# Transposing the next lane pair's x0 into DRAM ahead of the lane switch, in a Strassen cross-network kernel

## The chip, the cores and the metric

One core of one Trainium2 chip. The metric is the device time of one execution, in microseconds (us). The kernel before the change took 2412.36 us in the median of its first three runs (2412.25 to 2421.04).

## The reference

```python
B, F, D, L = 16384, 100, 16, 6          # Din = min(F * D, 1024) = 1024
# x0: (16384, 1024) bf16, ws: (6, 1024, 1024) bf16, bs: (6, 1024) bf16
def reference(x0, ws, bs):
    x = x0
    for l in range(6):
        proj = einsum('bd,de->be', x, ws[l]) + bs[l]
        x = x0 * proj + x
    return x
```

## The kernel before

The batch is cut into eight *lane pairs* (`lp`) of two *lanes* of 1024 rows. All six layers of a pair run with the activations transposed in SBUF: features on partitions, batch in the free dimension. A *unit* is one layer of one lane, so a pair has twelve units. Each layer's product is a Strassen scheme (seven half-size products, two of them split once more), fed by a ring of ten weight tiles of 512 KB each, nine per layer. Three of these nine are plain quarters of `ws`. The other six are sums that the first pair computes and stores in DRAM (`Lc`).

At the *lane switch* the last layer of a pair overlaps the first layer of the next. Each lane has four quarters of x0 (512 batch rows by 512 features, 512 KB). In the switch eight quarters of x0 come in and eight quarters of the result (`xf`) go out, each through a DMA transpose.

```python
def w_src(l, pid):                                   # where a weight tile is loaded from
    # ... pid 1, 2, 4: a quarter of ws[l], "(k p) e -> p k e": rows of 1 KB
    return Lc[l, CIDX[pid]].rearrange("p (k e) -> p k e", k=KH)     # rows of 4 KB

def prefetch():                                      # load as soon as a ring slot is free
    while st["next"] < len(keys) and can_alloc(st["next"]):
        # ...
        st["dma"] = nc.sync.dma_start(t_[:], w_src(key[1], key[2]))

def load_x0(lp, lane, eh, n):
    r0 = lp * LB + lane * PR + n * NB
    nc.sync.dma_start_transpose(out=q(x0L[lane], eh, n), in_=x0[r0:r0 + NB, eh * H:(eh + 1) * H])

def store_quarter(lp, lane, eh, n, xf):
    # ... dst = the quarter of xL
    nc.sync.dma_start_transpose(out=dst, in_=xf[:].rearrange("r j k p -> r (j k p)"))
    nc.sync.dma_start(out[...], q(xL[lane], eh, n)...)

def finish(c, add, eh, n):                           # a quarter of a layer is done
    tt(c, c, add, ADD)
    tt(c, c, q(x0T, eh, n), MULT)
    if nxt_x0:                                       # last layer, and a next pair exists
        load_x0(lp + 1, lane, eh, n)                 # x0T's quarter was read for the last time
    x_out(c, eh, n)                                  # last layer: makes xf, calls store_quarter
# ... tail_a does the same for a lane's last two quarters (eh = 1)
```

All these DMAs are issued by SyncE, in order. Only the accumulations `xL += c` of the middle layers come from GpSimd.

## Time and profile before

| | before |
|---|---|
| median of 3 runs | 2412.36 us |
| profiled span | 2414.6 us |
| mean distance of lane switches | 297.8 us |
| twelve undisturbed units (estimate, 12 x 23.4) | 281 us |
| TensorE at half clock, without the end of the run | 65 us |

The distance of switches is taken from the trace: from the first matmul that reads the new x0 in one pair to that in the next, mean of six. The half clock is the sum of the stretches at 0.5 in the trace's record of the granted clock.

The head of the profile's page gives the span, and each engine's busy time, its share and its instructions:

```profile
span 2414.6 us, 32963 instructions
PE 2286.9 (95%) x12912; PEld 1269.5 (53%) x12912; DVE 2116.1 (88%) x2096; ACT 1783.9 (74%) x2485; POOL 110.7 (5%) x133
```

The view of windows compares one switch with a steady stretch. Columns: the stretch and its length, busy us of each engine with its instructions, the granted clock, the mean busy share of the 16 DMA engines, GB/s. (The share counts packets' own times, which overlap a little, so a full engine shows about 1.0 to 1.2.)

```profile
core 0: us, PE busy (x) PEld busy (x) DVE busy (x) ACT busy (x) POOL busy (x), PEclk, DMA share, GB/s
577.70:645.20 67.50, 56.76 (x311) 30.70 (x310) 49.47 (x50) 43.00 (x61) 0.00 (x0) 0.95 1.02 241
400.00:590.00 190.00, 190.00 (x1108) 108.15 (x1107) 176.29 (x174) 150.95 (x212) 12.90 (x15) 1.00 0.58 154
```

In steady layers TensorE is busy all the time. In the switch it loses 11 of 67 us, and the DMA engines are full. The timeline of TensorE in that switch shows for which data it waited (in brackets: idle us before, and what ended it):

```profile
610.01 0.61 PE L259 MATMUL XB<-x0L,wp 128*128 128x256 bf16 x4 [1.26 <-DMA wp<-in_ws_dram]
612.49 0.61 PE L259 MATMUL XB<-ti,wp 128*128 128x256 bf16 x4 [1.86 <-DMA wp<-Lc]
...
620.41 1.04 PE L247 MATMUL XA<-x0L,wp 128*128 128x512 bf16 x4 [1.69 <-DMA wp<-Lc]
...
632.14 1.04 PE L259 MATMUL XB<-ti,wp 128*128 128x256 bf16 x4 [5.93 <-DMA wp<-Lc]
632.97 1.91 PE L247 MATMUL XA<-t,wp 128*128 128x512 bf16 x4
```

Every wait is for a weight tile. After the longest one, four 512-column matmuls take 1.91 us; at full clock the same four take 1.04 us. The timeline of the SyncE queue says where the weights were (start, us in the queue's hands, line, output<-input):

```profile
593.12 5.48 SPq L150 DMA_TRANSPOSE x0L<-in_x_dram  x2
598.70 4.56 SPq L155 DMA_TRANSPOSE xL<-xf  x2
...
604.20 0.49 SPq L100 DMA_DIRECT2D wp<-in_ws_dram  x1
...
606.00 2.07 SPq L100 DMA_DIRECT2D wp<-Lc  x2
608.17 5.33 SPq L150 DMA_TRANSPOSE x0L<-in_x_dram  x1
613.59 2.41 SPq L155 DMA_TRANSPOSE xL<-xf  x1
616.05 1.42 SPq L100 DMA_DIRECT2D wp<-Lc  x2
...
620.06 5.18 SPq L150 DMA_TRANSPOSE x0L<-in_x_dram  x1
625.34 2.43 SPq L155 DMA_TRANSPOSE xL<-xf  x1
627.86 1.02 SPq L100 DMA_DIRECT2D wp<-Lc  x2
```

A plain load leaves the queue in 0.5 to 1.0 us. A transpose holds it for 2.3 to 5.3 us, and the last weights that TensorE waits for are issued at 627.86, behind four transposes of x0 and four of `xf` in this list.

### The profile page before, as it was taken

The numbers are of one execution on the slowest core, as the hardware profiler recorded it, in microseconds if no ns is written. First come the engines' busy times: TensorE is split into PE (matmuls) and PEld (weight loads), VectorE is DVE, ScalarE is ACT, GpSimd is POOL, SyncE is SP. The second block draws the span as 40 slices with busy tenths as digits, with TensorE's granted clock in tenths as the row PEclk, the third lists the DMA queues.
The fourth block names the chain that finished last, engine by engine and source line by source line (L and its number), as shares of the span: only waits on it lengthen the run. The fifth ranks groups of instructions, "written<-read, shape, count | busy, mean of one in ns | idle before, by whom it ended". The sixth has DMA issues, their size and how long they took to land.

```text
span 2414.6 us, 32963 instructions
## 1 busy us (share of the span) xinstructions
PE 2286.9 (95%) x12912; PEld 1269.5 (53%) x12912; DVE 2116.1 (88%) x2096; ACT 1783.9 (74%) x2485; POOL 110.7 (5%) x133
## 2 busy tenths in 40 slices
PE   6999989999899997999989999899998999989997
PEld 3454545555455554555545555455554555545553
DVE  6998879998899988999879998799987999889997
ACT  4777767777677785787767887677776878768775
POOL 0000000000000000000000000000000000000000
PEclk9999999999999999999999999999999999999998
DMA  7465695557954579545784558845588456874566
GB/s 200 137 188 136 161 236 139 148 131 179 240 150 126 135 183 237 147 122 147 191 230 130 131 149 197 218 126 131 153 201 222 114 136 165 208 197 123 147 172 144
DMA packets 439899, 400.10 MB, mean 166 GB/s; under 512 B 276416, under 2 KB 386496, under 8 KB 439744
## 3 DMA queue, kind: packets, MB, share of 16 engines
q1 hardware_dynamic: 421312, 330.89, 49.0%
q0 software_dynamic: 18432, 67.12, 14.4%
q8 instruction: 101, 1.65, 0.3%
q14 instruction: 54, 0.44, 0.1%
HBM read 211.29 MB, written 52.43 MB: 109 GB/s over the span
## 4 chain that ended last, share of the span: by engine, by line
PE 77%; DVE 15%; DMA 5%; SPq 1%; issue 1%; ACT 1%; DVEq 0%; ACTq 0%
PE pA L247 35%; PE XA L247 23%; PE XB L259 19%; DVE t L63 4%; DVE D L63 3%; DVE ti L63 3%; DMA xL<-xf 3%; DMA x0L<-in_x_dram 2%; DVE S L63 2%; SPq L150 1%; DVE xf L63 1%; DVE xL L63 1%; DVE Q L63 1%; ACT P5s L239 1%; DMA wp<-in_ws_dram 0%
## 5 line engine op out<-in xcount | busy, mean ns | idle before, releaser
L247 PEld LDWEIGHTS <-wp 128*128 128x128 bf16 x7712 | 759.0, 99 | 773.8 <-issue 46.6
L247 PE MATMUL pA<-t,wp 128*128 128x512 bf16 x3104 | 780.2, 381 | 0.0
L259 PEld LDWEIGHTS <-wp 128*128 128x128 bf16 x5040 | 494.9, 99 | 333.8 <-DMA wp<-Lc 51.3
L239 ACT CAST F<-XB 128x1024 bf16<-128x1024 f32 x360 | 364.3, 1012 | 291.0 <-PE XB L259 284.4
L259 PE MATMUL XB<-ti,wp 128*128 128x256 bf16 x2880 | 436.9, 275 | 52.4 <-DMA wp<-Lc 45.5
L247 PE MATMUL XA<-t,wp 128*128 128x512 bf16 x1536 | 400.6, 385 | 2.4 <-DMA wp<-Lc 2.4
L247 PE MATMUL XA<-xL,wp 128*128 128x512 bf16 x1280 | 326.8, 379 | 2.3 <-ACT P5s L239 2.3
L247 PE MATMUL pA<-xL,wp 128*128 128x512 bf16 x1280 | 328.5, 379 | 0.0
L242 ACT ACTIVATE U3s<-pA,b_all 128x512 bf16<-128x512 f32 x384 | 264.4, 688 | 39.4 <-PE pA L247 19.0
L239 ACT CAST G<-XB 128x512 bf16<-128x512 f32 x360 | 211.7, 588 | 106.5 <-PE XB L259 105.2
L242 ACT ACTIVATE P1s<-pA,b_all 128x512 bf16<-128x512 f32 x384 | 266.0, 693 | 26.3 <-PE pA L247 18.5
L242 ACT ACTIVATE U2s<-pA,b_all 128x512 bf16<-128x512 f32 x384 | 266.1, 693 | 14.4 <-PE pA L247 5.1
L239 ACT CAST S<-XA 128x1024 bf16<-128x1024 f32 x192 | 194.3, 1012 | 64.1 <-PE XA L247 64.1
L239 ACT CAST P5s<-XA 128x1024 bf16<-128x1024 f32 x192 | 195.3, 1017 | 50.1 <-DVE D L63 30.8
L63 DVE TENSOR_TENSOR D<-D,x0L 128x4096 bf16<-128x4096 bf16 x96 | 220.0, 2292 | 13.3 <-ACT D L242 9.4
L63 DVE TENSOR_TENSOR t<-xL 128x4096 bf16<-128x4096 bf16 x80 | 183.4, 2293 | 23.4 <-DMA xL<-S 14.7
L63 DVE TENSOR_TENSOR t<-xL,t 128x2048 bf16<-128x2048 bf16 x160 | 194.9, 1218 | 0.0
L63 DVE TENSOR_TENSOR xL<-D,xL 128x4096 bf16<-128x4096 bf16 x64 | 146.7, 2292 | 6.6
L63 DVE TENSOR_TENSOR S<-S,U2s 128x2048 bf16<-128x2048 bf16 x96 | 117.2, 1221 | 31.8 <-ACT S L239 31.5
L305 POOL DMA_DIRECT2D xL<-Q x64 | 55.2, 863 | 1905.9 <-ACT U3s L242 862.2
L259 PE MATMUL XB<-t,wp 128*128 128x256 bf16 x1008 | 139.3, 275 | 0.0
L63 DVE TENSOR_TENSOR D<-P5s,U3s 128x2048 bf16<-128x2048 bf16 x96 | 117.3, 1222 | 24.4 <-ACT U3s L242 24.4
(43 smaller groups left out, 1752.0 us busy)
## 6 DMA issues: line engine op xcount, KB each, us to landing
wp<-Lc SPq DMA_DIRECT2D x252, 512.0 KB, 4.6
wp<-in_ws_dram SPq DMA_DIRECT2D x139, 512.0 KB, 5.9
xL<-Q POOLq DMA_DIRECT2D x64, 512.0 KB, 5.7
xL<-S POOLq DMA_DIRECT2D x64, 512.0 KB, 6.4
out_dram<-xL SPq DMA_DIRECT2D x64, 512.0 KB, 3.8
Lc<-wp SPq DMA_DIRECT2D x36, 512.0 KB, 5.0
w<-in_ws_dram SPq DMA_DIRECT2D x12, 512.0 KB, 7.7
x0L<-in_x_dram SPq DMA_TRANSPOSE x64, 5.4
```

The costliest lines, as they stand in the source:

```text
L63: return nc.vector.tensor_tensor(out=out, in0=in0, in1=in1, op=op)
L150: nc.sync.dma_start_transpose(out=q(x0L[lane], eh, n), in_=x0[r0:r0 + NB, eh * H:(eh + 1) * H])
L239: nc.scalar.copy(out=dst, in_=src)
L242: nc.scalar.activation(out=dst, in_=src, func=IDENT, bias=bias_col(eh, m), scale=1.0)
L247: nc.tensor.matmul(dst, lhsT=w_[:, k, m * P:(m + 1) * P], rhs=b_[:, k, :], start=(start and k == 0), stop=(k == KH - 1), skip_group_check= ...
L259: nc.tensor.matmul(dst[:, m * NQ:(m + 1) * NQ], lhsT=wv[:, k, m * P:(m + 1) * P], rhs=b_[:, k, :], start=(start and m == 0 and k == 0), st ...
L305: nc.gpsimd.dma_start(q(xst, eh, n), c, accum_op=ADD)
```

## The change

Intent: take the x0 transposes out of the switch. In layers 1 to 4 of each pair, each unit transposes one quarter of the next pair's x0 into an SBUF buffer and stores it in DRAM (`x0s`) in the layout that SBUF wants. The switch then only fetches 4 KB rows. Beside this, the weights 1, 2 and 4 are also copied into `Lc`, so that all later loads of weights read 4 KB rows. The staging pool gives up one buffer to make room. Core of the diff (pool and index changes and the startup's `w_save` cut):

```diff
+    x0s = dram.tile([2, 2, 2, 2, P, KH * NB], BF16, name="x0s")
...
+    def w_save(l, pid, t_):
+        nc.sync.dma_start(Lc[l, CIDX[pid]], t_[:].rearrange("p k e -> p (k e)"))
...
-            st["dma"] = nc.sync.dma_start(t_[:], w_src(key[1], key[2]))
+            if key[0] == 0:
+                nc.sync.dma_start(t_[:], w_src(key[1], key[2]))
+                if key[2] in (1, 2):
+                    w_save(key[1], key[2], t_)
+            else:
+                nc.sync.dma_start(t_[:].rearrange("p k e -> p (k e)"), Lc[key[1], CIDX[key[2]]])
...
+    def pre_x0(lp, lane, eh, n):
+        r0 = lp * LB + lane * PR + n * NB
+        xs = late["xf"].tile([P, KH, KH, P], BF16, name="xf")
+        nc.sync.dma_start_transpose(out=xs[:].rearrange("p a b r -> p a (b r)"), in_=x0[r0:r0 + NB, eh * H:(eh + 1) * H])
+        nc.sync.dma_start(x0s[lp % 2, lane, eh, n], xs[:].rearrange("p a b r -> p (a b r)"))
+
+    def fetch_x0(lp, lane, eh, n):
+        nc.sync.dma_start(q(x0L[lane], eh, n).rearrange("p k b -> p (k b)"), x0s[lp % 2, lane, eh, n])
...
             if nxt_x0:
-                load_x0(lp + 1, lane, eh, n)
+                fetch_x0(lp + 1, lane, eh, n)          # the same in tail_a
...
         prefetch()
+        if 1 <= l <= 4 and lp + 1 < NLP:
+            i_ = (l - 1) * 2 + lane
+            pre_x0(lp + 1, i_ // 4, i_ % 2, (i_ // 2) % 2)
```

More of the change, by code (lines that the diff above doesn't have):

```diff
@@ L49 @@
     stage = stage_ctx.enter_context(tc.tile_pool(name="stage", bufs=2))
-    late = {}
-    CIDX = {5: 0, 6: 1, 7: 2, 3: 3, "2i": 4, "4i": 5}
+    stage1 = stage_ctx.enter_context(tc.tile_pool(name="stage1", bufs=1))
+    late = {"xf": stage1}
+    CIDX = {5: 0, 6: 1, 7: 2, 3: 3, "2i": 4, "4i": 5, 1: 6, 2: 7, 4: 8}
     Lc = dram.tile([L, len(CIDX), P, KH * H], BF16, name="Lc")
+    x0s = dram.tile([2, 2, 2, 2, P, KH * NB], BF16, name="x0s")
     pA = [psum.tile([P, NB], FP32, name=f"pA{i}") for i in range(KH)]
@@ L73, in w_src @@
             return wl[H:D, H:D].rearrange("(k p) e -> p k e", p=P)
-        return Lc[l, CIDX[pid]].rearrange("p (k e) -> p k e", k=KH)
+        raise KeyError(pid)
+    def w_save(l, pid, t_):
+        nc.sync.dma_start(Lc[l, CIDX[pid]], t_[:].rearrange("p k e -> p (k e)"))
     USE = [1, 2, "2i", 5, 3, 6, 4, "4i", 7]
@@ L108, in load_stage @@
         nc.sync.dma_start(w22[l][:], w_src(l, 4))
-        w12[l] = stage.tile([P, KH, H], BF16, name="w12")
+        w_save(l, 4, w22[l])
+        w12[l] = stage1.tile([P, KH, H], BF16, name="w12")
         nc.sync.dma_start(w12[l][:], ws[l][0:H, H:D].rearrange("(k p) e -> p k e", p=P))
@@ L135, in combo @@
             tt(s_[7], a11, a21, SUB)
-        nc.sync.dma_start(Lc[l, CIDX[pid]].rearrange("p (k e) -> p k e", k=KH), t_[:])
+        w_save(l, pid, t_)
         if pid == "4i":
@@ L195 @@
     nc.sync.dma_start(t_[:], w_src(0, 1))
+    w_save(0, 1, t_)
     load_stage(0)
@@ L373, in tail_a @@
                 for n in (1, 0):
-                    load_x0(lp + 1, lane, 1, n)
+                    fetch_x0(lp + 1, lane, 1, n)
             if last_layer:
```

## The prediction

> **What bounds it now.** The table of engines has TensorE busy 2286.9 us of 2414.6. By stretches (windows), from 400 to 590 us and in every steady stretch like it TensorE is busy 190.0 of 190 us at full clock, VectorE about 176. One layer of one lane takes 23.4 us, twelve take 281. But in the chain of waits the lane switches (marked by the transposes back, `xL<-xf`, at 598.7, 1193.8, 1492.7, 1792.4 ...) come every 298 us: each of the seven loses about 17 us, some 120 in all. From 590 to 700 us TensorE is idle 12.4 us; the list of waits gives most of it to late weights (45.5 us behind `wp<-Lc` and 18.3 behind `wp<-in_ws_dram` in one group over the run, longest 7.8). Most of the rest is half clock after the gaps (four 512-column matmuls in 1.9 us instead of 1.03; one granted-clock stretch of 6.8 us at 0.5). That agrees with the Trainium skill, "TensorE: Matmul & The Clock Gate", Part 1: after an idle window of about 3.4 us the array runs at half rate.
>
> **Why the weights are late.** All transfers but the accumulations go through the one in-order SyncE queue. In its timeline the next lanes' nine weights, wanted from 591 us on, are issued from 604.2 to 630.2, behind transposes: those of x0 hold the queue 2.1 to 5.3 us each, 2.74 where two follow one another, those of `xf` 2.0 to 2.4. DMA's share is 0.95 to 1.13 from 589 to 632 us, so transfers are the limit too. Estimated occupancy of a switch: 8 x 2.74 (x0) + 8 x 2.35 (xf) + 17 x 1.5 (weights and stores, at the 350 GB/s that traced plain loads reach) = 66 us; the trace takes 577.7 to 645. (The skill, "DMA: Bandwidth & Descriptors", Latency and other measured facts, gives 261 GB/s for a transpose; this trace shows 190 to 225.)
>
> **What the change does.** Per switch, eight x0 transposes become plain 4 KB-row loads: 0.4 us of queue and about 1.4 of transfer each (estimate from `wp<-Lc`), so -11 us of DMA and -18 of queue. Three `in_ws` weights per layer become `Lc` rows (4.6 us to landing instead of 5.9): about -1.5 us. Added: a transpose and a 512 KB store in eight of twelve units, about +4.1 us of DMA per 23.4 us, where the share is 0.42 to 0.73, so it fits; 18 more `Lc` stores in the first lane pair, three near the start, where DMA is at 0.97.
>
> **On the path.** The switch stays near the DMA limit (about 54 us of traffic), so I expect 12 of its 17 us back: the long weight wait and the half clock behind it. 7 x 12 = -84. Against it: +3 at the start, +6 for accumulations delayed in steady layers (VectorE already waits up to 1.4 us for `xL<-S`, with 1.7 us slack a unit).
>
> **Predicted: 2337 us, range 2305 to 2380.** Faster by over 2%: 0.81; within 2%: 0.16; slower: 0.03.
>
> **Signs.** Switch period 298 -> about 286 us; TensorE's waits for `wp` from 76 us to under 30; half-clock stretches at switches mostly gone; steady stretches still 100% TensorE, DMA share up by about 0.15; nine weights issued before about 612 in switch time; VectorE's wait for `xL<-xf` (95 us) at least halved.
>
> **What would make it wrong.** A store waiting for its transpose to land holds weights up in steady layers; hoisted transposes fall into the switch's end; accumulations slowed so VectorE (93% busy) becomes the limit; or `xf`, not x0, holds the queue, and only 5 us per switch come back.

## More of the kernel before

The framework that builds the program chooses SyncE's order. It need not keep the program's order: a DMA that waits for little can be issued well ahead of its place, as the queue after the change will show. The order of TensorE, ScalarE and VectorE is fixed by the program.

## The result, and the profile after

The changed kernel took 2378.29 us in the median (2375.51 to 2379.37, four runs) against 2413.18 for the kernel before in the same rounds. The ratio is 0.9847, with a 95% interval of 0.9824 to 0.9869. A ratio here is the mean time of one kernel's runs over that of the other's of the same rounds, so it is not quite the ratio of the medians. The gain is 1.5%, about 35 us, where 75 us were predicted; the time lies just under the top of the predicted range of 2305 to 2380, and the class "faster by over 2%" was missed.

| | before | after |
|---|---|---|
| profiled span | 2414.6 us | 2373.7 us |
| first matmul starts | 11.1 us | 13.7 us |
| mean distance of lane switches | 297.8 us | 291.5 us |
| half clock, without the end of the run | 65 us | 41 us |

From the start of the second pair to the end, before took 2414.6 - 312.4 = 2102.2 us and after 2373.7 - 314.8 = 2058.9 us: 43.3 us less over seven switches, or 6.2 us each. The whole gain came from there. (The two profiled executions took 2416.68 and 2375.51 us, 6 us further apart than the medians; by the medians, with the later start added back, it is (34.9 + 2.6) / 7 = 5.4 us each.)

The head of the page after the change. (Of the matmuls 253 records are missing; the weight loads, x12912 as before, show that none was left out. Busy times of TensorE are therefore read 1 to 2% low.)

```profile
span 2373.7 us, 32873 instructions
PE 2264.8 (95%) x12659; PEld 1267.6 (53%) x12912; DVE 2114.4 (89%) x2096; ACT 1784.9 (75%) x2485; POOL 110.7 (5%) x133
```

Windows: the switch, the 54 us behind it, and a steady stretch, columns as above.

```profile
core 0: us, PE busy (x) PEld busy (x) DVE busy (x) ACT busy (x) POOL busy (x), PEclk, DMA share, GB/s
573.00:636.00 63.00, 56.40 (x306) 30.89 (x311) 51.31 (x52) 43.33 (x62) 0.00 (x0) 0.95 0.99 272
636.00:690.00 54.00, 53.16 (x305) 30.32 (x310) 52.76 (x54) 42.02 (x59) 1.72 (x2) 1.00 1.01 267
690.00:850.00 160.00, 158.97 (x910) 90.78 (x928) 146.67 (x147) 127.46 (x180) 12.03 (x14) 1.00 0.57 158
```

The switch is shorter but its DMA engines are as full as before (0.99). The transposes ahead are not spread over the layers as the program has them: they need nothing but a free buffer, so the queue runs all eight right behind the switch (share 1.01 from 636 to 690), and the steady stretch shows no extra traffic. TensorE is still busy for 53.2 of these 54 us.

TensorE's timeline in the switch, with its waits:

```profile
604.74 0.61 PE L281 MATMUL XB<-ti,wp 128*128 128x256 bf16 x4 [0.65 <-DMA wp<-Lc]
...
612.02 1.04 PE L269 MATMUL XA<-x0L,wp 128*128 128x512 bf16 x3 [1.04 <-DMA wp<-Lc]
...
622.41 1.04 PE L281 MATMUL XB<-ti,wp 128*128 128x256 bf16 x4 [4.59 <-DMA wp<-Lc]
623.24 1.91 PE L269 MATMUL XA<-t,wp 128*128 128x512 bf16 x4
```

The small waits shrank. The long one, for the weights of the same group, is still 4.6 us and still brings the half clock. The SyncE queue:

```profile
586.83 1.70 SPq L171 DMA_DIRECT2D x0L<-x0s  x2
588.94 6.49 SPq L176 DMA_TRANSPOSE xL<-xf  x2
...
598.42 2.09 SPq L110 DMA_DIRECT2D wp<-Lc  x2
600.60 0.40 SPq L171 DMA_DIRECT2D x0L<-x0s  x1
601.09 5.93 SPq L176 DMA_TRANSPOSE xL<-xf  x1
607.08 1.06 SPq L110 DMA_DIRECT2D wp<-Lc  x2
...
612.82 5.47 SPq L176 DMA_TRANSPOSE xL<-xf  x1
618.39 1.01 SPq L110 DMA_DIRECT2D wp<-Lc  x2
```

Where x0's transposes held the queue 5.2 to 5.3 us, `xf`'s now hold it 5.5 to 5.9, and before they took 2.4. The transpose of `xf` is the same instruction, so most of its 5.5 to 5.9 us is not its own cost. The reading that fits is back-pressure: the full DMA engines take a transpose only slowly, and the next one in line inherits that time. No run isolates this. Part of the queue's time did come back: in this switch the transposes and fetches of x0 together with the transposes of `xf` held it for 47.1 us before and 37.8 us after.

The packets of the trace give the DMA work of one switch: their times summed and divided by the 16 engines. (The window after holds part of a first transpose ahead.)

```
                            before 577 to 646            after 573 to 636
256 B packets (transposes)  32768, 44.8 us = 16 x 2.80   17580, 24.0 us
1 KB packets                 4824, 15.6 us                3584, 11.8 us = 7 x 1.68
4 KB packets                  768,  8.9 us                2176, 26.3 us = 17 x 1.55
```

So 512 KB cost 2.80 us as a transpose and 1.55 us as 4 KB rows. A whole switch (eight quarters in, eight out, eight stores, nine weights) comes to about 72 us before and 62 us after.

### The profile page after: what moved, and what is told of

Read it like the earlier page. It is cut to its first block, busy times and chain, and to the rows that moved or that the text cites. A ratio compares the mean times of both kernels' runs of the same rounds, so it can differ in the third digit from the quotient of the medians.

```text
span 2373.7 us, 32873 instructions
## 1 busy us (share of the span) xinstructions
PE 2264.8 (95%) x12659; PEld 1267.6 (53%) x12912; DVE 2114.4 (89%) x2096; ACT 1784.9 (75%) x2485; POOL 110.7 (5%) x133
## 4 chain that ended last, share of the span: by engine, by line
PE 75%; DVE 15%; DMA 6%; issue 2%; ACT 1%; SPq 1%; DVEq 0%; ACTq 0%; POOLq 0%
PE pA L269 34%; PE XA L269 22%; PE XB L281 18%; DVE t L65 4%; DMA xL<-xf 4%; DVE D L65 3%; DVE ti L65 3%; DVE S L65 2%; DMA x0L<-x0s 1%; DVE xL L65 1%; DVE Q L65 1%; DVE xf L65 1%; SPq L161 0%; DMA xL<-S 0%; DMA wp<-Lc 0%
## 5 line engine op out<-in xcount | busy, mean ns | idle before, releaser
L269 PE MATMUL pA<-t,wp 128*128 128x512 bf16 x2982 | 758.7, 381 | 6.4
L269 PE MATMUL XA<-t,wp 128*128 128x512 bf16 x1474 | 386.1, 385 | 3.7 <-DMA wp<-Lc 0.5
L269 PE MATMUL pA<-xL,wp 128*128 128x512 bf16 x1254 | 323.2, 379 | 1.3
L65 DVE TENSOR_TENSOR t<-xL 128x4096 bf16<-128x4096 bf16 x80 | 183.4, 2293 | 41.6 <-DMA xL<-S 28.5
L65 DVE TENSOR_TENSOR Q<-Q,P1s 128x2048 bf16<-128x2048 bf16 x96 | 117.6, 1225 | 19.7 <-ACT Q L261 10.9
```

Of the source, the lines that this page charges most:

```text
L65: return nc.vector.tensor_tensor(out=out, in0=in0, in1=in1, op=op)
L269: nc.tensor.matmul(dst, lhsT=w_[:, k, m * P:(m + 1) * P], rhs=b_[:, k, :], start=(start and k == 0), stop=(k == KH - 1), skip_group_check= ...
```

## The experiments

The theories, as they stood before the first run. **A (order):** weights are late because they stand in the in-order queue behind transposes that are slow or not ready. **B (DMA work):** the switch is as long as the DMA engines need for its transfers; order only decides who waits. **C:** the transposes ahead, run right behind the switch, eat part of the gain. "Period" is the mean distance of switches; medians are given with that of the kernel before in the same rounds.

### The weight copies alone, and x0 alone

The first is the change with `load_x0` in place of `fetch_x0` and no `pre_x0`:

```diff
-                fetch_x0(lp + 1, lane, eh, n)
+                load_x0(lp + 1, lane, eh, n)        # the same in tail_a; pre_x0 and x0s removed
```

> The kernel before with one part of the change alone: all nine weights per layer come from the row copies; x0 is still transposed in the switch. Theory A (weights stand in the in-order queue behind transposes that are not ready, so the moment of issue decides): the x0 transposes are still there, nearly nothing comes back, 2400 to 2415 us, switch period 296 to 298 us. Theory B (the DMA engines are full in the switch): only about 1.5 us of traffic per switch goes, about 2400 us. Both say that this part is small; if more than 15 us come from it, both are wrong about x0.

Measured: 2414.86 us (before 2415.09), ratio 1.0001 [0.9987, 1.0016], period 297.5. The 4 KB rows for three of nine weights gave nothing.

The second is the change with weights 1, 2 and 4 read from `ws` as before, and no copies of them:

```diff
-                nc.sync.dma_start(t_[:].rearrange("p k e -> p (k e)"), Lc[key[1], CIDX[key[2]]])
+                if key[2] in (1, 2, 4):
+                    nc.sync.dma_start(t_[:], w_src(key[1], key[2]))
+                else:
+                    nc.sync.dma_start(t_[:].rearrange("p k e -> p (k e)"), Lc[key[1], CIDX[key[2]]])
```

> The change without its weight copies: x0 is transposed ahead and fetched as rows, weights 1, 2 and 4 come from the input in 1 KB pieces as before. Theories A and B: nearly the whole gain stays, 2375 to 2390 us, period 292 to 294 us. The sum of the gains of this run and of the rows-only run should be near the 35 us of the whole change.

Measured: 2377.07 us (before 2415.09), ratio 0.9842 [0.9825, 0.9858], period 292.2. The whole gain is x0's.

### No transposes ahead after the first pair (wrong result)

```diff
-        if 1 <= l <= 4 and lp + 1 < NLP:
+        if 1 <= l <= 4 and lp == 0:                  # and fetch_x0 always reads x0s[1, ...]
```

> The change, but only the first lane pair transposes x0 ahead; later switches fetch the same stale rows, so the result is wrong on purpose. All added steady traffic of the later pairs is gone, the switch itself is unchanged. Theory C (the transposes ahead, which the queue runs in the 50 us right after the switch, eat part of the gain): period 288 to 290 us, 2355 to 2365 us. Theories A and B: the time is lost in the switch, period stays at 292 us, 2372 to 2380 us.

Measured: 2376.63 us (before 2415.09), period 291.6; the result is wrong, as meant. Removing the added transposes and stores from six of the seven pairs that have them gives nothing back. Theory C falls: they are free where they run.

### The switch's weights from the GpSimd queue

```diff
-                nc.sync.dma_start(t_[:].rearrange("p k e -> p (k e)"), Lc[key[1], CIDX[key[2]]])
+                eng = nc.gpsimd if key[1] == 0 else nc.sync
+                eng.dma_start(t_[:].rearrange("p k e -> p (k e)"), Lc[key[1], CIDX[key[2]]])
```

> The change, but the nine weights that a switch needs (first layer of each later lane pair) are issued from the GpSimd queue, which has no other work there, so that they no longer stand behind the transposes of xf. The bytes moved are the same. Theory A (order): the 4.6 us wait at the tenth group and the half clock after it go, weights are issued when their slot comes free, period 284 to 287 us, 2325 to 2345 us. Theory B (DMA engines full, share 0.97 to 1.02 from the switch's start): issuing earlier only delays something else, period 290 to 293, 2365 to 2385 us.

Measured: 2469.83 us (before 2415.09), ratio 1.0218 [1.0192, 1.0244], period 304.2. Neither theory expected a loss of this size. The weights did go out early, eight of them from 601.5 to 616.7 us, and took 11.8 us to land (the median of all 63 in the run). The SyncE queue and VectorE in that stretch:

```profile
602.42 22.26 SPq L177 DMA_TRANSPOSE xL<-xf  x2
```

```profile
625.62 1.23 DVE L65 TENSOR_TENSOR xf<-Q,xL 128x2048 bf16<-128x2048 bf16 x1 [17.63 <-DMA xL<-xf]
```

Two transposes in a row, which hold the queue 4.4 to 7.3 us in the same switch of the kernels before and after, held on for 22.3 us while the other queue's 4 KB packets went through. VectorE waited 17.6 us for the buffer that they read, and TensorE then for VectorE. The bytes were the same, so serving one transfer earlier made another late, which is what B says. It is not the whole loss: from 602.4 to 625 us the packets themselves took longer, 45 ns for 256 B and 254 ns for 4 KB, against 22 and 193 ns in the switch of the change. The loss also shows that the choice matters: of the two, the transposes were the wrong ones to keep waiting. The Trainium skill, "DMA: Bandwidth & Descriptors", Issuing engines are not separate DMA queues, says that another issuing engine only saves the time to issue. This run agrees that it brings no bandwidth, and shows that it can do harm, 13 us a switch against the change.

### Output stores from the GpSimd queue

```diff
-        nc.sync.dma_start(out[...]...)               # in store_quarter
+        nc.gpsimd.dma_start(out[...]...)
```

> The change, but the output stores are issued from the GpSimd queue, which is idle in a switch, so that the SyncE queue no longer stands about 8 us per switch waiting for a transpose to land before a store. Same bytes. Theory A: weights are issued some 5 us earlier, the wait at the tenth group shrinks by half or more, 2345 to 2365 us. Theory B: no gain, 2370 to 2390 us, or a loss, as stores from another queue take their turns beside the transposes, as the weights of the earlier run did.

Measured: 2412.64 us (before 2414.43), ratio 0.9998, period 297.3. A's expectation fails. SyncE no longer waits for a transpose to land, but its transposes now hold the queue 8.3 us each in lane 1, with the stores running beside them. The gain of the change is gone.

### Three buffers of xf

```diff
-            late["xf"] = ctx.enter_context(tc.tile_pool(name="xfp", bufs=2))
+            late["xf"] = ctx.enter_context(tc.tile_pool(name="xfp", bufs=3))
```

> The change with three buffers of xf in place of two, so that VectorE waits less for a transpose to have read its buffer (59.5 us of such waits in the run). Same bytes, same queue. Theory A (head of the queue waits for VectorE, VectorE for buffers): 2345 to 2368 us. Theory B: the transposes get no faster, 2370 to 2382 us.

Measured: 2376.17 us (before 2414.43), period 291.2. No gain: VectorE's waits for a buffer were not what holds the switch.

### Each fetch twice

```diff
+        for _ in range(2):
             nc.sync.dma_start(q(x0L[lane], eh, n)..., x0s[lp % 2, lane, eh, n])
```

> The change, but each x0 fetch in a switch is issued twice (same bytes, same place, right result). It adds about 8 x 1.55 = 12 us of DMA work and 8 x 0.4 = 3 us of queue to each switch. Theory B (DMA work sets the length): period +7 to +12 us, 2425 to 2460 us, slower than the kernel before the change or like it. Theory A (queue order and waits for VectorE set it): +0 to +3 us a switch, 2380 to 2400 us.

Measured: 2477.99 us (before 2414.43), ratio 1.0257, period 305.5, which is 14 us more than the change. That is on B's side but above its range, and the run was not clean: the second fetch writes what the first one wrote, so it has to wait for it, and the order of the queue changed too: at the start of the switch the second fetch leaves behind the next transpose, at 594.04 us against 589.63 us for the first. Hence the next two.

### One extra plain store per quarter, and half of each fetch

The extra store reads the same `xf` buffer as the transpose, so it adds DMA work and no wait (three `xf` buffers, so the run with three buffers is its base):

```diff
     def store_quarter(lp, lane, eh, n, xf):
+        if lp + 1 < NLP:
+            nc.sync.dma_start(xos[lp % 2, lane, eh, n], xf[:].rearrange("r j k p -> r (j k p)"))
```

> The change with three xf buffers (the earlier run with three buffers, 2376 us, is its base) and, beside every transpose back of the first seven lane pairs, one plain store of the same xf buffer into unused DRAM. It becomes ready with the transpose, so it brings no new wait into the queue, only 0.4 us of queue and about 1.55 us of DMA work, eight times a switch, 12 us in all. (The run with fetches issued twice was not clean: the second fetch had to wait for the first.) Theory B (the switch is as long as its DMA work): period +7 to +13 us, 2425 to 2470 us. Theory A (order and waits of the queue): +0 to +3.5 us a switch, 2376 to 2400 us.

Measured: 2438.4 us (before 2416.85), ratio 1.0088 [1.0071, 1.0105], period 300.5: 9.3 us a switch for 12.4 us of DMA work (8 x 1.55).

The half fetch takes DMA work away and leaves every instruction in place:

```diff
-        nc.sync.dma_start(q(x0L[lane], eh, n).rearrange("p k b -> p (k b)"), x0s[lp % 2, lane, eh, n])
+        nc.sync.dma_start(q(x0L[lane], eh, n).rearrange("p k b -> p (k b)")[:, 0:KH * NB // 2],
+                          x0s[lp % 2, lane, eh, n][:, 0:KH * NB // 2])
```

> The change, but each fetch brings only half of each row, so x0 of later pairs is half stale and the result is wrong on purpose. Number of instructions, order and waits of the queue stay; 8 x 0.78 = 6 us of DMA work per switch go. Theory B: period -3 to -6 us, 2335 to 2357 us. Theory A: 0 to -1.5 us, 2367 to 2378 us.

Measured: 2346.1 us (before 2416.85), ratio 0.9707 [0.9692, 0.9721], period 287.3: 4.2 us a switch less, for 6.2 us of DMA work. Its output is wrong, which doesn't matter for the time. Both runs fall in B's range and outside A's. The DMA work of the switch sets its length. The long wait in the switch at 600 us, 4.59 us in the change, moved with it, to 6.34 us with the extra stores and 3.17 us with the half fetches:

```profile
642.38 1.03 PE L285 MATMUL XB<-ti,wp 128*128 128x256 bf16 x4 [6.34 <-DMA wp<-Lc]
```

```profile
618.23 0.61 PE L281 MATMUL XB<-ti,wp 128*128 128x256 bf16 x4 [3.17 <-DMA wp<-Lc]
```

No run tells whether the DMA engines themselves or the memory behind them set the packets' times.

### Which quarters count

The same extra store, but beside the first two, the middle four, or the last two transposes of a switch:

```diff
-        if lp + 1 < NLP:
+        if lp + 1 < NLP and lane == 0 and eh == 0:     # first two
+        if lp + 1 < NLP and lane != eh:                # middle four
+        if lp + 1 < NLP and lane == 1 and eh == 1:     # last two
```

> Base: the change with three xf buffers, 2376 us. One extra store (1.55 us of DMA) beside the first two transposes back of each switch only, those of lane 0's first half, where the DMA engines still have gaps. If DMA work counts only from the moment that the engines are full until the last late weight has landed: +0 to +1.5 us a switch, 2374 to 2388 us. If all DMA work of the switch counts alike: +2.2 us a switch (a quarter of the 8.9 us of the run with eight stores), 2390 us or more.

> Extra stores beside the four middle transposes only (lane 0's second half, lane 1's first half), which stand ahead of the late weights while the engines are full. By position: nearly all of what eight stores cost, +6 to +9 us a switch, 2418 to 2440 us. If all work counts alike: +4.5 us a switch, 2403 to 2412 us.

> Extra stores beside the last two transposes only (lane 1's second half), which are issued after the last late weight. By position: +0 to +1 us a switch, 2374 to 2384 us. If all work counts alike: +2.2 us a switch, 2390 us or more.

Measured in one set of rounds (before 2415.08). The base is the earlier run with three buffers (2376.17 us, period 291.2, before 2414.43):

| extra stores | DMA work added | median | period | per us of DMA work |
|---|---|---|---|---|
| first two | 3.1 us | 2395.15 us | 294.1 (+2.9) | 0.9 |
| middle four | 6.2 us | 2422.87 us | 298.0 (+6.8) | 1.1 |
| last two | 3.1 us | 2378.80 us | 292.1 (+0.9) | 0.3 |

The last two count little, as expected: they are issued after the last late weights. The middle four count fully. The expectation for the first two was wrong: although the DMA engines still have gaps there (share 0.75 from 573 to 587 us in the change), work added there costs nearly as much as in the middle. There the other expectation held, that all work counts alike.

### The other half: park the result and transpose it later

If DMA work is the limit, the eight transposes of `xf` can go the same way as those of x0:

```diff
+    def post_out(lp, lane, eh, n):
+        r0 = lp * LB + lane * PR + n * NB
+        xo = late["xf"].tile([P, KH, KH, P], BF16, name="xf")
+        nc.sync.dma_start_transpose(out=xo[:].rearrange("p a b r -> p (a b) r"), in_=xos[lp % 2, lane, eh, n])
+        nc.sync.dma_start(out[r0:r0 + NB, eh * H:(eh + 1) * H].rearrange("(j p) d -> p j d", p=P),
+                          xo[:].rearrange("p a b r -> p a (b r)"))
     def store_quarter(lp, lane, eh, n, xf):
+        if lp + 1 < NLP:
+            nc.sync.dma_start(xos[lp % 2, lane, eh, n], xf[:].rearrange("r j k p -> r (j k p)"))
+            return
...
+        if 1 <= l <= 4 and lp > 0:
+            i_ = (l - 1) * 2 + lane
+            post_out(lp - 1, i_ // 4, i_ % 2, (i_ // 2) % 2)
```

> The change carried to the other half of the switch: for all but the last lane pair the result is parked untransposed in DRAM as 4 KB rows, and its transpose and output store run later, in the steady layers of the next pair. By packet times that takes about 8 x 2.9 us of DMA out of the switch (a transpose of 2.8 and a store of 1.7 us become one store of 1.55). Theory B (the switch is as long as its DMA work): the switch falls below its limit, period 282 to 285 us, 2315 to 2335 us. Theory A (order in the queue alone) also expects a gain, since the transposes that are waited for go. A rival: the extra 36 us of DMA after the switch delay weights and accumulations there, 2350 us or more.

Measured: 2425.15 us (before 2414.43), ratio 1.0046 [0.9993, 1.0099], period 302.3 (the first of its six distances is 318, the others 297 to 301), right result. The switch itself lost its waits: from 600 to 660 us TensorE is busy 59.6 of 60. The time went to the layers behind it. TensorE and the SyncE queue there:

```profile
742.52 1.03 PE L293 MATMUL XB<-xL,wp 128*128 128x256 bf16 x4 [13.97 <-DMA wp<-Lc]
```

```profile
723.88 4.97 SPq L178 DMA_TRANSPOSE xf<-xos  x1
728.89 0.58 SPq L168 DMA_DIRECT2D x0s<-xf  x1
732.45 0.39 SPq L179 DMA_DIRECT2D out_dram<-xf  x1
736.04 2.17 SPq L167 DMA_TRANSPOSE xf<-in_x_dram  x1
738.25 1.05 SPq L110 DMA_DIRECT2D wp<-Lc  x2
```

Sixteen transposes that had no reason to wait were issued as one long chain (each waits for a buffer, each store for its transpose), and the weights of a whole layer stood behind it until 738 us. Here the order of the queue matters, as theory A says, but not alone: the DMA engines are full there too (share 1.04 from 660 to 700 us, 1.01 from 700 to 742). The work fills the engines, and the order makes the weights the last of it.

### The same, with the transposes pinned to their units

The next edit spreads the work over the layers. It changes the order of the queue and the crowding of the DMA engines together, and no run separates the two. VectorE's order is fixed by the program. A two-column memset by VectorE on the buffer makes the transpose wait for its unit:

```diff
         xs = late["xf"].tile([P, KH, KH, P], BF16, name="xf")
+        nc.vector.memset(xs[:, 0, 0, 0:2], 0.0)        # the same for xo in post_out
```

> The kernel with both transposes out of the switch (the run that parked the result), which lost its gain to a 14 us wait in the second layer, where sixteen transposes that had been ready early stood in the queue ahead of that layer's weights. Here a two-column memset by VectorE, whose order is fixed, opens each buffer, so that one transpose back and one ahead run per unit. If the switch is free of waits and the loss came from the hoisting alone: period 281 to 284 us, 2300 to 2325 us. If the DMA work in steady layers (share about 0.9) delays accumulations or weights: 2330 to 2380 us.

Measured: 2322.8 us (before 2416.85), ratio 0.9607 [0.9589, 0.9625], period 282.9. As expected.

With three `xf` buffers and `post_out` moved from the start of a unit to its middle (behind the first `finish`):

> As the pinned kernel, with three xf buffers and the transposes back opened in the middle of a unit, those ahead at its start, so that the DMA work is spread. Within 10 us of the pinned kernel; faster only if that one shows waits at the starts of units.

Measured: 2313.07 us (before 2416.85), ratio 0.957 [0.9555, 0.9584], period 281.8, right result. This beats both kernels. Windows of its switch and of the layers behind it:

```profile
core 0: us, PE busy (x) PEld busy (x) DVE busy (x) ACT busy (x) POOL busy (x), PEclk, DMA share, GB/s
590.00:660.00 70.00, 69.12 (x396) 39.31 (x403) 66.93 (x69) 54.99 (x77) 0.00 (x0) 1.00 0.64 225
660.00:850.00 190.00, 188.85 (x1085) 108.11 (x1105) 176.58 (x188) 151.60 (x213) 13.75 (x16) 1.00 0.91 229
```

The DMA share is 0.64 in the switch and 0.91 behind it, and TensorE is busy in both (what is missing is mostly missing records). The switch's DMA work is now 25 x 1.55 = 39 us, less than the 47 us of its two units.

## Why the prediction was wrong, point by point

- **What bounds the kernel:** right. Steady layers are TensorE's, the loss is in seven switches, and it is late weights and the half clock behind them. The undisturbed period of 281 us that was estimated is the one that the last kernel reached (281.8).
- **"those of x0 hold the queue 2.1 to 5.3 us each ... -18 of queue":** this was read wrongly as a cost of the instruction. After the change the transposes of `xf` hold the queue 5.5 to 5.9 us in x0's place, and in the switch shown 9.3 us of queue came back (47.1 to 37.8), not 18. The reading that fits is the full DMA engines pushing back, so this time should not be counted as a second gain beside the DMA work.
- **"The switch stays near the DMA limit (about 54 us of traffic), so I expect 12 of its 17 us back":** this is the step that failed. The mechanism was right (extra store +9.3, half fetch -4.2 us a switch), but the term was mis-sized: 6.2 us by the traces, 5.4 by the medians. Three parts of it are shown. The -1.5 us for the weights were worth nothing (the weight copies alone: ratio 1.0001). The -11 us of x0 were 10 by packets (8 x (2.80 - 1.55)). And not all eight quarters count: the last two, issued behind the last late weights, cost 0.3 us per us of work where the first six cost about 1.0. Applied to the change that leaves an estimate of 6 x 1.25 + 2 x 1.25 x 0.3 = 8 us. The half fetch, which takes work away at the very places of x0, gave 4.2 / 6.2 = 0.7 us per us, which makes an estimate of 7 us. The remaining 1 to 2 us a switch stay open: the replacement also changes the order of the queue, and no run separated that.
- **The switch's limit was also taken too low.** By packets the traffic was 72 us before and 62 after, not 66 and 54. The switch was still far above the 47 us of its two units. So the long wait stayed at 4.6 us, and with it the half clock: 41 us of 65 remained, where "mostly gone" was predicted.
- **"+3 at the start":** right, the first matmul came 2.6 us later. **"+6 for accumulations delayed":** not found, the kernel without most of the added traffic runs as fast (2376.6 against 2378.3). VectorE's waits for `xL<-S` did grow, from 14.7 to 28.5 us over the run, but they are 32.1 us in that kernel too.
- **"DMA share up by about 0.15" in steady layers:** wrong. The transposes ahead ran in the 54 us behind the switch instead. That was listed as a risk; here it did no harm, and with twice as many transposes it brought a wait of 14 us behind the switch shown.
- **The other signs:** TensorE's waits for `wp` fell from 76 us to 45, not to under 30; the ninth weight of the switch was issued at 621 us, not before about 612; VectorE's wait for `xL<-xf` fell from 95 to 60 us, not to half.
- **The last risk listed, that only 5 us per switch come back because `xf` holds the queue,** is close to what happened in size, and `xf` did hold the queue. But what sets the size is DMA work rather than the queue, so the number is met partly by luck.

In sum: 7 x 12 = 84 us were expected from the switches; 7 x 6.2 = 43 came by the traces, 37 by the medians.

## What to carry to other kernels

Where DMA engines are full, cost a stretch in engine time per transfer (packets times their duration), and count only what stands ahead of the last transfer that something waits for; do not count time at the head of an in-order queue as well, since the next instruction may inherit it, as `xf` did here. Here each us of DMA work taken out of the full stretch shortened it by about 0.6 to 0.7 us, and the stall disappeared only in the kernels whose remaining work (39 us) fitted under the compute beside it (47 us). Work that is moved to a quiet place needs a dependency that keeps it there: here the work that was ready early was issued early, ahead of what mattered.

## What the Trainium skill lacked or had wrong

- "DMA: Bandwidth & Descriptors", Latency and other measured facts: it gives 261 GB/s for a DMA transpose with a non-contiguous middle dimension, and about 350 to 400 for the contiguous case. Neither was reached. Here 512 KB took 2.80 us of engine time (2048 packets of 256 B, 22 ns each), which is 187 GB/s; 4 KB rows took 1.55 us, 338 GB/s.
- The same page, Queues, rings and completion order, says that an engine takes turns between queues packet by packet. It does not say what that does to a transpose with its small packets beside another queue's large ones: two transposes held the queue 22.3 us beside eight 512 KB loads from GpSimd, against 4.4 to 7.3 us without them.
- The same page, Issuing engines are not separate DMA queues, calls issuing from several engines a matter of issue time. Here it cost 13 us a switch with weights and 6 us with output stores, with the transposes held up (22.3 us for two, 8.3 us for one).
- "Perfetto Trace Analysis", DMA Instruction — HWDGE, lacks a number for how long a transpose's span in the queue becomes while the DMA engines are full: 2.4 us before and 5.5 to 5.9 us after, for the same instruction.
- "TensorE: Matmul & The Clock Gate", Part 1, gives half rate after an idle window of about 3.4 us. Waits of 4.6 and 5.9 us agree (four matmuls took 1.91 us behind them, 1.04 us otherwise). But two waits of only 2.7 us in the run after the change (ended at 1484.5 and 1500.5 us) were also followed by 3.4 us of half clock each, so less idle time than that was enough.
